# A 128x320 float32 memset on GpSimd behind each gather of an edge-featured message-passing layer

## The chip, the cores and the metric

The kernel runs on one core of a Trainium2 chip. The time is device microseconds of one execution, the median over runs. The engines are called as in the profile: PE (TensorE), PEld (its weight loads), DVE (VectorE), ACT (ScalarE), POOL (GpSimd) and SP (SyncE, which here only issues DMAs).

## The reference

A message-passing layer on a graph of N = 12,500 nodes and E = 800,000 edges, with 64 features per node, 4 per edge, and a hidden width H = 128. `src` and `dst` are random.

```
h_src = x[src]
h_dst = x[dst]
m_in = concatenate([h_src, h_dst, e_attr], axis=-1)     # 132 wide
h = silu(m_in @ w1 + b1)                                # 128 wide
msg = h @ w2 + b2                                       # 64 wide
return segment_sum(msg, dst, N)
```

## The kernel before

The node halves of `m_in @ w1` are made once: `Atab`, a table in DRAM with one row of 256 float16 numbers for each source node (512 bytes: two halves that are added up, for precision), and `Btab` in SBUF for the target nodes. For an edge there remain a row of `Atab`, a row of `Btab`, four edge features times a small matrix, the silu, and the sum by target. The product with `w2` is made after the sum, once for each node.

So that the sum needs no scatter, edges are put in order of their target first. `rank` works out each edge's place and `place` writes records of 16 edges to a DRAM buffer `buf` by an indirect DMA on GpSimd (the "scatter", L944 `buf<-cb,idx`, some 400 of them). The edges come in 16 portions; `rank` and `place` of the next portion run as a *filler* inside the main loop over the present one. The last portions' loop has no filler left.

The main loop (`run`) has 1590 iterations of 512 edges each, four tiles of 128. Work for one iteration is spread over several of them, with these lags: `load` of the records' target and source numbers 11 iterations ahead, `pairs` 10, `sources` (DVE makes the row numbers `ix`) 8, `gather` 6, `spread` 4, `targets` (ACT) 2, `marks` (DVE) 1, then in the iteration itself `pre` and `silu`, and `onehot` 1 and `seg` and `accum` 2 behind. In detail:

- `gather(n)`, L1155, issues four indirect DMAs on GpSimd's queue. Each fetches 128 rows of 512 bytes from `Atab` into `ga[:, t, :]`. `ga` has seven buffers (`NGA`), so the gather for iteration n + 6 needs the buffer that `pre(n - 1)` has read.
- `pre(n)` on PE: for each of the four tiles one matmul with the edge features (L1143) and two with `Btab` (L1145), then two of 512 columns that add the gathered rows by an identity matrix (L1147). All go into one PSUM bank `px`, of which there are three.
- `silu(n)` on ACT, L1166, reads `px` and writes `h`.
- `seg(n - 2)` on PE, L1174, sums `h` by target with a one-hot matrix `sg` (float32, made by ACT at L1162 from `ob`), into another `px`; `accum`, L1182, adds this on DVE to `S`.
- `targets`, L1118 and L1119 on ACT, and L1128 on DVE prepare the one-hot matrices, for two iterations at a time.

The filler's lines that show in the rows are L477, L492, L579, L583 and L591 (`rank`), L927 to L986 (`place`: DVE makes `mk` and `oh`, PE packs records in L983 and L986, ACT copies them to `cb` in L958, GpSimd scatters them).

The order of the work on each engine is the order in which the program is written; `in_order` sets what within an iteration goes first, on all engines alike. GpSimd does, in the main loop, nothing but the gathers and the scatters. DMAs on its queue take turns on eight semaphores, so that a DMA waits until the one eight places before it has landed.

Of the kernel before, what the change touches and what calls it, by code (L numbers as in the profile page):

```python
# [10 lines left out]
F32 = mybir.dt.float32  # L11
# [70 lines left out]
def tile_mpnn(ctx, tc, x, e_attr, src, dst, w1, b1, w2, b2, out, portions):  # L82
# [8 lines left out]
    VE, SC, GP, PE = nc.vector, nc.scalar, nc.gpsimd, nc.tensor  # L91
# [18 lines left out]
    cst = ctx.enter_context(tc.tile_pool(name="cst", bufs=1))  # L110
# [709 lines left out]
    def records(p, c0, cn):  # L820
# [53 lines left out]
        p["rec", c0] = (pay, lo, hv)  # L874
        yield 1200

    below = [zero[:, :CS * PC], zero[:, :CS * PC]]

    def place(p):
# [271 lines left out]
    def gather(n):  # L1151
        s = st[n]
        ga = wk.tile([128, 4, 2 * H], FH, name="ga", bufs=NGA)
        for t in range(4):
            GP.indirect_dma_start(out=ga[:, t, :], out_offset=None, in_=Atab,  # L1155
                                  in_offset=bass.IndirectOffsetOnAxis(ap=s["ix"][:, t:t + 1], axis=0))
        s["ga"] = ga

    def onehot(n):
# [33 lines left out]
    def run(m0, m1, filler):  # L1193
# [4 lines left out]
        for n in range(m0 - LL, m1 + 2):  # L1198
# [20 lines left out]
            if on(LG):  # L1219
                gather(n + LG)  # L1220
# [204 lines left out]
```

## Time and profile before

| | |
|---|---|
| median of three runs | 11,197.96 us (11,196.83 to 11,198.25) |
| span of the profiled execution | 11,179.7 us |
| that execution's time, with 18.3 us around the span as in the median | about 11,198 us |
| loop: first to last gather | 317.8 to 11,106.5 us |
| busy: PE, DVE, ACT, POOL | 73%, 57%, 35%, 58% |
| gathers | 6360, 951 ns mean |
| DMA, mean | 70 GB/s, 777 MB moved |

Before 317.8 us the tables and the first portion are made; behind the loop, some 70 us, the product with `w2` and the output. In the loop the profile shows the same picture slice by slice; up to about 1700 us DVE is the busiest engine, and from about 10,100 us on only gathers, `pre`, `silu`, `seg` and `accum` are left.

In a row of the time view the columns are: start in us, length, engine, line, operation, output and inputs, and in brackets the idle time of the engine before it with the instruction that ended it. "issue" means that the engine waited for nothing the profile shows, "remote" that the releaser isn't known. A row of a group has instructions, busy time, mean ns of one, then idle time before them and what ended it. In a row of a stretch each engine has its busy time and count, and then come the clock granted to PE, the DMA share and GB/s. The recorded ends of matmuls are modelled.

### The profile page before, as it was taken

Reading aid. Unit: us, or ns where it says so; the run is one execution under the profiler, and the core shown is the slowest. Engines: PE = TensorE matmul, PEld = TensorE weight load, DVE = VectorE, ACT = ScalarE, POOL = GpSimd, SP = SyncE. Lnnn points to the kernel's source line nnn. Section 1 sums busy time; section 2 is a strip of 40 time slices with the busy share of each in tenths; the row PEclk is TensorE's granted clock in tenths of the full one; section 3 lists DMA queues with packets and bytes.
Section 4 is the critical chain, followed back from the end, with each engine's and each line's share of the span. In section 5 each row is a group of like instructions: output and inputs, shape, how many; then the busy total and the mean of one; then the engine's idle time right before and its main releaser. Section 6 shows DMA issues by size and latency. Waiting matters only on the chain. (4 is left out here: it accounts for less than half of the span.)

```text
span 11179.7 us, 214957 instructions
## 1 busy us (share of the span) xinstructions
PE 8116.8 (73%) x73739; PEld 6653.7 (60%) x73739; DVE 6365.6 (57%) x18821; ACT 3859.6 (35%) x5331; POOL 6499.4 (58%) x6828
## 2 busy tenths in 40 slices
PE   7677777777777777777777777777777777775556
PEld 5566666666666566566566566666565565554445
DVE  8666676666665555555655555655555665441112
ACT  3233333333333333333333333333333333333333
POOL 1555555555555665566655666566566566666664
PEclk8777888888888778888888888888788887877777
DMA  2334434443443444444444444444444444444444
GB/s 92 64 66 72 67 58 71 65 73 64 72 66 64 76 67 66 76 68 67 77 66 66 76 68 66 74 69 68 75 67 66 74 67 69 69 67 71 72 72 68
DMA packets 3427360, 777.19 MB, mean 70 GB/s; under 512 B 3152950, under 2 KB 3215334, under 8 KB 3425036
## 3 DMA queue, kind: packets, MB, share of 16 engines
q1 hardware_dynamic: 3206638, 316.00, 26.1%
q0 software_dynamic: 218016, 446.07, 15.1%
q8 instruction: 645, 10.57, 0.4%
q14 instruction: 399, 3.27, 0.1%
q10 hardware_dynamic: 1662, 1.29, 0.0%
HBM read 712.51 MB, written 54.08 MB: 69 GB/s over the span
## 5 line engine op out<-in xcount | busy, mean ns | idle before, releaser
L1155 POOL DMA_INDIRECT ga<-Atab,ix x6360 | 6050.6, 951 | 4120.9 <-issue 1511.7
L1166 ACT ACTIVATE h<-px 128x512 f32<-128x512 f32 x1590 | 946.7, 595 | 6596.1 <-remote 2752.7
L1174 PE MATMUL px<-h,sg 128*128 128x129 f32 x12720 | 2375.2, 337 | 928.6 <-issue 387.7
L1174 PEld LDWEIGHTS px<-h,sg 128*128 128x128 f32 x12720 | 2065.8, 240 | 1155.0 <-issue 533.8
L983 PE MATMUL pl<-mk,oh 128*128 128x160 f16 x18750 | 1987.5, 260 | 575.8 <-issue 493.3
L983 PEld LDWEIGHTS <-oh 128*128 128x128 bf16 x18750 | 1637.8, 110 | 1037.3 <-issue 767.7
L1145 PE MATMUL px<-Btab,oT 128*128 x12720 | 1731.0, 249 | 159.4 <-issue 154.0
L1143 PE MATMUL px<-WE,pts 65*128 65x128 bf16 x6360 | 1489.0, 250 | 383.5 <-issue 241.1
L1182 DVE TENSOR_TENSOR S<-S,px 128x129 f32 x3180 | 906.2, 285 | 1341.2 <-remote 562.5
L1145 PEld LDWEIGHTS <-oT 128*128 128x128 bf16 x12720 | 1233.0, 114 | 575.1 <-issue 523.4
L930 DVE TENSOR_TENSOR mk<-fix,pay 128x320 int32<-128x320 int32 x1563 | 758.1, 485 | 1322.5 <-remote 712.0
L937 DVE TENSOR_TENSOR oh<-fix,lo 128x1536 bf16<-128x1536 bf16 x1563 | 1482.4, 948 | 0.1
L1147 PE MATMUL px<-ga,idA 128*128 128x512 f16 x3180 | 1172.0, 454 | 51.6 <-issue 46.2
L591 DVE TENSOR_REDUCE slT<-rx 128x5 f32<-128x490 f32 (+1 forms) x1302 | 833.2, 642 | 614.1 <-remote 305.1
L1119 ACT ACTIVATE oT<-oT,scl 128x1024 bf16<-128x1024 bf16 x795 | 986.1, 1240 | 26.7
L1162 ACT ACTIVATE sg<-ob 128x512 f32<-128x512 bf16 x1590 | 982.1, 618 | 0.0
L1118 ACT ACTIVATE oT<-oT,nip 128x1024 bf16<-128x1024 f16 x795 | 906.9, 1141 | 31.6 <-DMA oT<-dsc 24.7
L1143 PEld LDWEIGHTS <-pts 65*128 65x128 f16 x6360 | 722.2, 114 | 159.6 <-issue 113.1
L583 PEld LDWEIGHTS <-selB 99*128 99x128 bf16 x6250 | 479.1, 108 | 539.7 <-issue 428.3
L1128 DVE TENSOR_TENSOR ob<-fix,d 128x1024 bf16<-128x1024 bf16 x795 | 550.1, 692 | 352.3 <-ACT sg L1162 164.8
L583 PE MATMUL rx<-bT,selB 99*128 99x98 bf16 x6250 | 598.4, 224 | 198.1 <-issue 189.1
L579 PE MATMUL rx<-ohb,triO 128*128 128x490 bf16 (+1 forms) x1302 | 541.6, 416 | 120.5 <-DVE slT L591 49.8
(326 smaller groups left out, 5973.1 us busy)
## 6 DMA issues: line engine op xcount, KB each, us to landing
oT<-dsc SPq DMA_DIRECT2D x795, 256.0 KB
ga<-Atab,ix POOLq DMA_INDIRECT x6360
pts<-buf SPq DMA_DIRECT2D x2385, 16.0 KB
buf<-zero SPq DMA_DIRECT2D x184, 120.0 KB
dsc<-buf SPq DMA_DIRECT2D x795, 4.0 KB
pld<-dsc SPq DMA_DIRECT2D x795, 4.0 KB
Btab<-in_e_attr_dram POOLq DMA_DIRECT2D x10, 1250.0 KB
el<-in_e_attr_dram SPq DMA_DIRECT2D x74, 160.0 KB
```

Source lines behind the costliest of these rows:

```text
L583: PE.matmul(xp[:EP, i * R:(i + 1) * R], selB[:NR, s_:s_ + 1].to_broadcast([NR, EP]), bT[g][:NR, :R], start=False, stop=i == n - 1)
L937: VE.tensor_tensor(oh[:EP, :sn].rearrange("p s (j t) -> p s j t", t=2), io3[:EP].rearrange("p (j t) -> p j t", t=2).unsqueeze(1).to_broadc ...
L983: PE.matmul(pa[:, u * CS * PC:(u + 1) * CS * PC], oh_[:, u * 128:(u + 1) * 128], mv, start=s0 + i + u == 0, stop=False)
L1118: SC.activation(oT, oT.bitcast(FH), AF.Abs, bias=nip1[:, 0:1])
L1119: SC.activation(oT, oT, AF.Relu, scale=scl[:, 2:3], bias=inv)
L1143: PE.matmul(pr[:, sl], s["pts"][:, sl], WE, start=t == 0, stop=False)
L1145: PE.matmul(pr[:, sl], s["oT"][:, sl], Btab[:, ds(v[t // 2], 1), u, :], start=False, stop=False)
L1147: PE.matmul(pr.rearrange("p (t h) -> p t h", t=4), idA, s["ga"][:, :, u * H:(u + 1) * H], start=False, stop=u == 1)
L1155: GP.indirect_dma_start(out=ga[:, t, :], out_offset=None, in_=Atab, in_offset=bass.IndirectOffsetOnAxis(ap=s["ix"][:, t:t + 1], axis=0))
L1162: SC.activation(sg, s["ob"][:, :4].rearrange("p t h -> p (t h)"), AF.Copy)
L1166: SC.activation(hs[n % 3][:, :, :H], st[n]["pr"].rearrange("p (t h) -> p t h", t=4), AF.Silu)
L1174: PE.matmul(s["so"][t // 2], s["sg"][:, t * 128:(t + 1) * 128], hs[n % 3][:, t, :], start=t % 2 == 0, stop=t % 2 == 1)
```

## The change

A float32 tile of 128 partitions by 320 elements, `idle`, is added to SBUF, and behind each of the four indirect DMAs of `gather` GpSimd clears it. No instruction reads the tile. 6360 memsets are executed in all. Lines behind the first insertion move down by one, those behind the second by two: the gather is then L1156, the memset L1158.

```diff
@@ -874,6 +874,7 @@
         p["rec", c0] = (pay, lo, hv)
         yield 1200
 
+    idle = cst.tile([128, 320], F32, name="idle")
     below = [zero[:, :CS * PC], zero[:, :CS * PC]]
 
     def place(p):
@@ -1154,6 +1155,7 @@
         for t in range(4):
             GP.indirect_dma_start(out=ga[:, t, :], out_offset=None, in_=Atab,
                                   in_offset=bass.IndirectOffsetOnAxis(ap=s["ix"][:, t:t + 1], axis=0))
+            GP.memset(idle, 0.0)
         s["ga"] = ga
 
     def onehot(n):
```

## The prediction

> **What bounds the kernel now.** I read the page first (busy shares), then who waited for whom, then GpSimd's own rows in order of time, and last the sums by stage.
>
> ```profile
> PE 8116.8 (73%) x73739; PEld 6653.7 (60%) x73739; DVE 6365.6 (57%) x18821; ACT 3859.6 (35%) x5331; POOL 6499.4 (58%) x6828
> L1155 POOL DMA_INDIRECT ga<-Atab,ix x6360 | 6050.6, 951 | 4120.9 <-issue 1511.7 <-remote 862.2 <-PE px L1147 759.5
> L944 POOL DMA_INDIRECT buf<-cb,idx x407 | 413.7, 1016 | 305.4 <-ACT cb L958 181.9 <-issue 111.3 <-DMA Atab<-S 9.7
> L1155 POOL DMA_INDIRECT ga<-Atab,ix x6360: 942/947/1623, 317.8 to 11106.5; - x199
> ```
>
> No engine is full. The last row is of the gathers alone (min/median/max in ns, first and last start in us). The page would let GpSimd (POOL) be called idle 42% of the time, but of its idle time 1511.7 us is "issue", the gap that stands before nearly every gather and in which nothing else can start. The gathers run from 317.8 to 11106.5 us: 10,789 us for 1590 iterations, 6.79 each. The waits:
>
> ```profile
> ACT h L1166 <- remote: 2752.7, 611, 10.0
> ACT h L1166 <- PE px L1147: 1959.4, 344, 26.3
> POOL ga L1155 <- issue: 1511.7, 4896, 4.9
> POOL ga L1155 <- remote: 862.2, 545, 3.0
> POOL ga L1155 <- PE px L1147: 759.5, 235, 11.4
>   PEld L1147: 4.8, 8
>   PE px L1147: 3.6, 4
> ```
>
> The last two rows are from the gather's line, of those who waited for it: nearly nobody, 12 times in 6360. So the gathered data is always early, six iterations ahead. The rows above say the opposite of GpSimd: 4896 gathers follow the one before them on the queue, and the other 6360 - 4896 = 1464 had to be let go by another engine. That makes 1464 bursts of DMAs with a pause behind each. Bursts of four, five (the fifth is a scatter of the filler) and eight, in GpSimd's rows by time (start, length, engine and line, idle time before):
>
> ```profile
> 6002.61 0.97 POOL L1155 DMA_INDIRECT ga<-Atab,ix  x1 [1.38 <-PE rx L583]
> 6003.88 0.95 POOL L1155 DMA_INDIRECT ga<-Atab,ix  x1 [0.30 <-issue]
> ...
> 6006.38 0.94 POOL L1155 DMA_INDIRECT ga<-Atab,ix  x1 [0.30 <-issue]
> 6008.77 0.94 POOL L1155 DMA_INDIRECT ga<-Atab,ix  x1 [1.45 <-PE pl L983]
> ...
> 6014.84 0.95 POOL L1155 DMA_INDIRECT ga<-Atab,ix  x1 [1.37 <-remote]
> ...
> 6019.84 1.01 POOL L944 DMA_INDIRECT buf<-cb,idx  x1 [0.30 <-issue]
> 6022.27 0.97 POOL L1155 DMA_INDIRECT ga<-Atab,ix  x1 [1.42 <-remote]
> ...
> 6082.04 0.95 POOL L1155 DMA_INDIRECT ga<-Atab,ix  x1 [1.35 <-remote]
> ...
> 6090.79 0.94 POOL L1155 DMA_INDIRECT ga<-Atab,ix  x1 [0.30 <-issue]
> 6093.88 0.94 POOL L1155 DMA_INDIRECT ga<-Atab,ix  x1 [2.14 <-remote]
> ...
> 10919.07 0.95 POOL L1155 DMA_INDIRECT ga<-Atab,ix  x1 [0.31 <-issue]
> 10922.06 0.95 POOL L1155 DMA_INDIRECT ga<-Atab,ix  x1 [2.04 <-remote]
> ...
> 10930.82 0.95 POOL L1155 DMA_INDIRECT ga<-Atab,ix  x1 [0.30 <-issue]
> 10933.76 0.94 POOL L1155 DMA_INDIRECT ga<-Atab,ix  x1 [1.99 <-remote]
> ```
>
> Inside a burst the starts are 1.25 us apart (0.95 + 0.30). From the start of a burst to the start of the next: four DMAs 6.16 and 6.07 us, five 7.43, eight 11.84, and eight in the tail 11.70. Four DMAs more cost 11.84 - 6.07 = 5.77, so 1.44 us for each, not 1.25, and T(n) = 1.44 n + 0.32 fits all (6.08, 7.52, 11.84). Over the loop it gives (6360 + some 380 scatters) x 1.44 + 1464 x 0.32 = 10,170 of the 10,789 us, 94%. So the loop keeps the time of GpSimd's DMAs, at 1.44 us each, though GpSimd itself shows 1.25. What lies between is in the next rows, of the last stretch, where the filler is over:
>
> ```profile
> 10919.58 0.59 PE L1147 MATMUL px<-ga,idA 128*128 128x512 f16 x2
> 10921.82 0.60 ACT L1166 ACTIVATE h<-px 128x512 f32<-128x512 f32 x1 [7.31 <-remote]
> 300.00:1700.00 1400.00, 1033.37 (x10345) 857.56 (x10343) 956.86 (x2961) 439.21 (x600) 770.25 (x807) 0.80 0.40 66
> 10300.00:11100.00 800.00, 451.42 (x3041) 385.09 (x3038) 153.28 (x493) 296.83 (x405) 513.23 (x542) 0.73 0.48 72
> ```
>
> TensorE (PE) is recorded to end the pre-activations at 10920.17, yet ACT's silu, which needs them, starts at 10921.82, and the next burst of gathers, which needs the same signal (the buffer is free), 0.24 us after the silu. The signal comes only 2.75 us after the last DMA of the burst has started (10919.07). In the last row, of the tail, PE is busy 451 of 800 us, DVE 153, ACT 297, POOL 513: nobody is full, and the period still follows the count of DMAs. The trace does not show what holds PE's signal back during a burst; it shows by how much. The first row of the two, 300 to 1700 us, is the one stretch where DVE is busier (957 of 1400 us) than POOL.
>
> **The change part by part.** 1. One tile of 320 float32 in each partition is added in SBUF; nothing reads it, so no engine gains a wait for it. 2. 6360 memsets are added on GpSimd's queue. On that queue, in the middle of the loop, the gathers of an iteration and the first of the next stood thus (a wait for DMASW is for the DMA eight places back, for PE_49 the buffer's last reader):
>
> ```order
> L1155 DMA ga<-Atab,ix 128x256 [waits DMASW3_49,PE_49]
> L1155 DMA ga<-Atab,ix 128x256 [waits DMASW4_49]
> L1155 DMA ga<-Atab,ix 128x256 [waits DMASW5_49]
> L1155 DMA ga<-Atab,ix 128x256 [waits DMASW6_49]
> L1155 DMA ga<-Atab,ix 128x256 [waits DMASW7_49,DVE_49,PE_49]
> ```
>
> and stand now, with a scatter (L945) behind them:
>
> ```order
> L1156 DMA ga<-Atab,ix 128x256 [waits DMASW1_49,DVE_49,PE_49]
> L1158 MEMSET idle 128x320 [waits Pool_49]
> L1156 DMA ga<-Atab,ix 128x256 [waits DMASW2_49]
> L1158 MEMSET idle 128x320 [waits Pool_49]
> L1156 DMA ga<-Atab,ix 128x256 [waits DMASW3_49]
> L1158 MEMSET idle 128x320 [waits Pool_49]
> L1156 DMA ga<-Atab,ix 128x256 [waits DMASW4_49]
> L1158 MEMSET idle 128x320 [waits Pool_49]
> L945 DMA buf<-cb,idx 76544x160 [waits DMASW5_49,Activation_49]
> ```
>
> Nothing changes places; a memset stands between any two gathers, and it waits only for the memset before it, which was done a whole DMA earlier. Behind it on the queue wait the next gather or the scatter. The price of a memset is bounded by GpSimd's own:
>
> ```profile
> L356 POOL MEMSET sg<- 1x512 f32 x24 | 12.8, 537 | 138.6 <-PE px L362 134.6 <-PE fix L193 3.9
> L356 POOL MEMSET sg<- 1x256 f32 x1 | 0.3, 306 | 3.3 <-PE px L362 3.3
> L373 POOL MEMSET S<- 128x1806 f32 x7 | 11.3, 1609 | 0.4
> 260.98 0.97 POOL L944 DMA_INDIRECT buf<-cb,idx  x1 [9.65 <-DMA Atab<-S]
> 261.99 1.61 POOL L373 MEMSET S<- 128x1806 f32 x1
> 0.30 0.12 POOL L1409 MEMSET const-bfloat16-1.0<- 128x1 bf16 x1
> 0.33 0.12 POOL L1409 MEMSET const-uint8-127<- 128x1 uint8 x1
> ```
>
> From 256 to 1806 elements is 1.303 us, 0.84 ns for an element, so 320 take 0.306 + 64 x 0.84 ns = 0.36 us (by the 512 row at most 0.37). 6360 of them are 2,280 us of GpSimd. A memset begins 0.04 us behind a DMA (261.95 to 261.99). What the trace never shows is a DMA that is ready behind a memset. The spacing s of gathers is then, as a low bound, 0.95 + 0.04 + 0.36 = 1.35, if the 0.30 of "issue" passes while the memset runs (the last two rows show such overlap: memsets of 0.12 us start 0.03 apart); as a high bound that plus 0.30, 1.65. I take 1.25 + 0.355 = 1.605: the gap stands before each indirect DMA but not before a memset, so it seems to belong to the DMA's own start.
>
> The forecast rests on what 1.605 does to the 1.44. It is more than 1.44, so DMAs no longer pile up. What held PE's signal is then the last DMA alone: T'(n) = (n-1) s + 1.44 + 0.32. Against T(n) each burst loses (n-1)(s - 1.44), and over the loop that is the 4896 gathers that follow another: 4896 x 0.165 = +808 us. From that I take off the stretch up to 1700 us, where DVE is fuller than POOL: 807 of 6828 GpSimd instructions, 12%. That leaves +711; the memset behind the last gather of a burst costs nothing, since it lies in the pause (1.4 to 2.1 us idle); if the pause went, it would cost its 0.36 as well, 1464 x 0.36 = 527. PE does not wait for later data: a whole burst that is late by 1.4 us comes out of a lead of six iterations, some 40 us. What is late next is the silu, which the pause feeds, and behind it PE's segment sums and DVE's adds.
>
> The profiled span is 11,179.7 us and the median of the runs 11,198; the 18.3 lie around the span and are kept. 11,198 + 711 = 11,909; I say 11,900.
>
> One more cost is possible. 300 to 1700 us holds some 750 gathers; if each memset held DVE up by its full 0.36 whenever DVE is busy (957/1400 = 0.68), the stretch would grow by 750 x 0.36 x 0.68 = +184. I leave it out: the gathers' 942/947/1623 shows a median 5 ns over the minimum beside a DVE that is busy 57%, so nothing on GpSimd is being held by DVE as a rule. The Trainium skill's page "SBUF — State Buffer" (section "SBUF: two separate sides") does say that GpSimd and a DVE instruction in a two-port mode exclude each other for a whole instruction; by that rule the sum would be nearer 12,090, and no row here shows such a hold on either side.
>
> **The rivals.** R1, all of it adds: PE's signal waits for GpSimd's whole chain, and each memset lengthens it. For: the 1.44 is more than GpSimd's own 1.25, so there is a serial thing that POOL's time may be added to. Against: the 0.19 that it exceeds looks like a second, parallel limit. 4896 x 0.36 = 1,760 (the last of a burst hidden) to 6360 x 0.36 = 2,290, less 12%: +1,550 to +2,010, 12,750 to 13,210.
>
> R2, the other side: with s over 1.44 there is a short calm behind each DMA, PE's signal slips through within the burst, and the pauses of 1.4 to 2.1 us go. GpSimd then runs without a break: 4 x 1.605 + 0.256 x 1.31 (407 scatters over 1590 iterations) = 6.76 per iteration, 10,740 us for 10,789 now: -50, 11,150. It decides at s = 1.61: below, faster (at 1.55, -400 at most, if PE and DVE can follow), above, slower (at 1.65, +235). Small waits that remain would push it up. For: a lone DMA is no pile. Against: in the tail each burst holds the signal although PE is recorded to have ended 1.65 us before.
>
> R3, no change: s is 1.35 to 1.44, the memset lies in the issue gap, and the 1.44 per DMA goes on setting the period: 11,198, up to +100.
>
> R4: the memset costs far more beside DVE or beside a descriptor write than alone: over 0.5 us each, above 13,200.
>
> **How the numbers follow.** Forecast 0.38; R1 0.20; R2 0.20, half of it below zero; R3 0.15; R4 0.07. Faster by over 0.2% (22 us, about what can be told from no change): 0.10, from R2. Within 0.2%: R3 mostly, and a little of R2, 0.13. Slower: 0.77. The forecast alone, with s from 1.54 to 1.65, is 4896 x 0.88 x (0.10 to 0.21) = +430 to +905, 11,630 to 12,100. The range for 8 in 10 runs from 11,130 (most of R2) to 13,000 (the lower half of R1).
>
> **What would show it.** GpSimd's rows: gather to gather 1.6 us with a memset of 0.36 behind each. Right: bursts of four take 6.5 to 6.6 us, eight 13.0, pauses remain, and silu starts some 1.7 us after the last gather. R1: four take 7.2 or more. R2: pauses vanish, the "remote" and PE waits before the gather fall to a few hundred us, and POOL is busy 75% or more of the span. R3: spacing 1.35 to 1.44 and bursts of four still 6.1. The prediction is wrong if memsets are longer than 0.4 us, if the gap before a gather shrinks, or if PE's signal no longer follows the DMAs.

## The result and the profile after

The changed kernel takes 10,956.7 us (10,948 to 10,966, four runs) where the kernel before takes 11,198.1 us: ratio 0.979, interval 0.978 to 0.980. It is 2.1% faster. The forecast was 11,900 us, slower, in a range that began at 11,130. Of all executions in this document one is left out of its ratio, as far slower than the others of its kernel: 16,097 us, of `w360` below.

The page's first row and the groups of GpSimd in the kernel after:

```profile
span 10946.3 us, 221318 instructions
PE 8233.5 (75%) x73739; PEld 6563.2 (60%) x73739; DVE 6642.0 (61%) x18821; ACT 3876.8 (35%) x5331; POOL 8972.5 (82%) x13188
L1156 POOL DMA_INDIRECT ga<-Atab,ix x6360 | 6100.6, 959 | 1491.9 <-issue 924.3 <-PE px L1148 253.2 <-remote 82.0
L1158 POOL MEMSET idle<- 128x320 f32 x6360 | 2438.4, 383 | 4.7
```

GpSimd's busy time grew by 2,473 us, nearly all of it the memsets, and its idle time before gathers fell by 2,629 us, from 4,120.9 to 1,491.9. So more idle time went than the memsets cost. Of it 587 us is "issue" (1511.7 to 924.3), a gap that is shorter behind a memset; the rest is pauses that other engines end, and these are the part to read: "remote" was 862.2 and is 82.0, PE's `px` was 759.5 and is 253.2. The waits, of GpSimd and of PE, in the kernel after:

```profile
POOL ga L1156 <- issue: 924.3, 5444, 4.9
POOL ga L1156 <- PE px L1148: 253.2, 150, 9.7
ACT h L1168 <- remote: 1466.4, 326, 15.4
PE px L1148 <- DMA ga<-Atab,ix: 407.4, 157, 6.2
```

5444 gathers now follow the one before on the queue, so 6360 - 5444 = 916 had to be let go by another engine, for 1464 before. Most of the 916 hardly wait: counted in the traces, waits of over 0.6 us before a DMA of this queue fell from 1368 to 257. The last row is new: PE waits for gathered data, 157 times. GpSimd has become the bound in a part of the loop. GpSimd's rows in the middle of the loop and in the tail:

```profile
6007.44 0.95 POOL L1156 DMA_INDIRECT ga<-Atab,ix  x1 [0.33 <-PE rx L783]
6008.40 0.38 POOL L1158 MEMSET idle<- 128x320 f32 x1
6008.94 0.95 POOL L1156 DMA_INDIRECT ga<-Atab,ix  x1 [0.16 <-issue]
6009.89 0.38 POOL L1158 MEMSET idle<- 128x320 f32 x1
6010.43 0.95 POOL L1156 DMA_INDIRECT ga<-Atab,ix  x1 [0.16 <-issue]
...
6013.43 1.00 POOL L945 DMA_INDIRECT buf<-cb,idx  x1 [0.17 <-issue]
6014.74 0.96 POOL L1156 DMA_INDIRECT ga<-Atab,ix  x1 [0.30 <-issue]
...
6021.06 0.95 POOL L1156 DMA_INDIRECT ga<-Atab,ix  x1 [0.49 <-remote]
...
10600.31 0.95 POOL L1156 DMA_INDIRECT ga<-Atab,ix  x1 [0.16 <-issue]
...
10606.29 0.95 POOL L1156 DMA_INDIRECT ga<-Atab,ix  x1 [0.16 <-issue]
```

Gathers start 1.495 us apart: 0.95, a memset of 0.38, and a gap of 0.16 that was 0.30 between two DMAs. The burst of five (6007.44 to 6014.74) takes 7.30 us, for 7.43 before, with no wait behind its scatter; the burst of four behind it 6.32, for 6.07 to 6.16. The tail runs at GpSimd's own 5.98 us an iteration, a little slower than before (11.70 / 2 = 5.85).

The plainest place is the first burst of the loop, 16 gathers in a row, while PE and DVE work on `rank` beside it: PE writes `rx` (L583), DVE reduces it (L591). In the kernel before:

```profile
326.46 0.61 PE L583 MATMUL rx<-bT,selB 99*128 99x98 bf16 x5
327.05 0.67 DVE L591 TENSOR_REDUCE slT<-rx 128x5 f32<-128x490 f32 x1 [1.41 <-PE rx L583]
328.13 0.61 PE L583 MATMUL rx<-bT,selB 99*128 99x98 bf16 x5
335.59 0.67 DVE L591 TENSOR_REDUCE slT<-rx 128x5 f32<-128x490 f32 x1 [7.55 <-issue]
336.31 0.57 PE L579 MATMUL rx<-ohb,triO 128*128 128x490 bf16 x1 [7.56 <-DVE slT L591]
336.67 0.61 PE L583 MATMUL rx<-bT,selB 99*128 99x98 bf16 x5
340.52 0.67 DVE L591 TENSOR_REDUCE slT<-rx 128x5 f32<-128x490 f32 x1 [3.94 <-remote]
```

and in the kernel after:

```profile
325.37 0.61 PE L583 MATMUL rx<-bT,selB 99*128 99x98 bf16 x5
326.09 0.66 DVE L591 TENSOR_REDUCE slT<-rx 128x5 f32<-128x490 f32 x1
326.27 0.61 PE L583 MATMUL rx<-bT,selB 99*128 99x98 bf16 x5
327.06 0.66 DVE L591 TENSOR_REDUCE slT<-rx 128x5 f32<-128x490 f32 x1
328.13 0.61 PE L583 MATMUL rx<-bT,selB 99*128 99x98 bf16 x5
328.85 0.66 DVE L591 TENSOR_REDUCE slT<-rx 128x5 f32<-128x490 f32 x1
```

The matmuls that end at 328.74 are seen by DVE at 335.59 before and at 328.85 after, in the middle of the same burst. PE is not behind with its own work there: it stands idle for 7.56 us, waiting for DVE. The other way round there is no delay: DVE's reduction ends at 336.26 and PE starts at 336.31. What comes late, when GpSimd's gathers follow each other at 1.25 us, is what PE signals.

The traces also record when a semaphore changed, for nine in ten of PE's signals and for about half of DVE's and ACT's. From 330 us on, the recorded signals of DVE come 0.011 us and those of ACT 0.009 us (medians) behind the end of an instruction that signals, in both kernels; those not recorded can't be judged by this. Those of PE come 1.06 us behind it in the median before and 0.56 after; 28% are over 2 us late before, 14% after, and 22% and 23% come within 0.05 us. So the change shortens the hold on PE's signals and does not end it.

### The profile page after: what moved, and what is told of

The parts are those of the page before. It is cut to its first block, busy times and chain, and to the rows that moved or that the text cites. A ratio compares the mean times of both kernels' runs of the same rounds, so it can differ in the third digit from the quotient of the medians.

```text
span 10946.3 us, 221318 instructions
## 1 busy us (share of the span) xinstructions
PE 8233.5 (75%) x73739; PEld 6563.2 (60%) x73739; DVE 6642.0 (61%) x18821; ACT 3876.8 (35%) x5331; POOL 8972.5 (82%) x13188
## 5 line engine op out<-in xcount | busy, mean ns | idle before, releaser
L1156 POOL DMA_INDIRECT ga<-Atab,ix x6360 | 6100.6, 959 | 1491.9 <-issue 924.3
L1176 PE MATMUL px<-h,sg 128*128 128x129 f32 x12720 | 2328.7, 333 | 368.2 <-issue 181.6
L1158 POOL MEMSET idle<- 128x320 f32 x6360 | 2438.4, 383 | 4.7
L1176 PEld LDWEIGHTS px<-h,sg 128*128 128x128 f32 x12720 | 2040.5, 237 | 576.5 <-issue 336.4
L984 PEld LDWEIGHTS <-oh 128*128 128x128 bf16 x18750 | 1589.1, 109 | 891.6 <-issue 594.2
L1146 PE MATMUL px<-Btab,oT 128*128 x12720 | 1771.7, 247 | 155.4 <-issue 142.5
L591 DVE TENSOR_REDUCE slT<-rx 128x5 f32<-128x490 f32 (+1 forms) x1302 | 834.0, 642 | 630.7 <-PE px L1148 241.3
L583 PEld LDWEIGHTS <-selB 99*128 99x128 bf16 x6250 | 458.9, 105 | 497.6 <-issue 381.6
```

The costliest lines, as they stand in the source:

```text
L984: PE.matmul(pa[:, u * CS * PC:(u + 1) * CS * PC], oh_[:, u * 128:(u + 1) * 128], mv, start=s0 + i + u == 0, stop=False)
L1146: PE.matmul(pr[:, sl], s["oT"][:, sl], Btab[:, ds(v[t // 2], 1), u, :], start=False, stop=False)
L1158: GP.memset(idle, 0.0)
L1176: PE.matmul(s["so"][t // 2], s["sg"][:, t * 128:(t + 1) * 128], hs[n % 3][:, t, :], start=t % 2 == 0, stop=t % 2 == 1)
```

## The experiments

Each was timed against the kernel before on its own chip; ratios are to that.

**The width of the memset.** Theory A: the spacing of the gathers is what counts. Theory B: any instruction behind a DMA lets the signals out.

```diff
-    idle = cst.tile([128, 320], F32, name="idle")
+    idle = cst.tile([128, 1], F32, name="idle")        # w1; 160, 240, 480, 360 in the others
```

> The memset clears 128x1 instead of 128x320; 6360 of them as before. Theory A (spacing): what helps is that the starts of two gathers lie 1.495 us apart and no longer 1.25, longer than the 1.44 us per DMA by which PE's signals were held. A memset of 0.1 us leaves the spacing at 1.20 to 1.30, so DMAs pile up as in the kernel before: 11,150 to 11,230 us, bursts of four 6.1 us from start to start. Theory B (presence): any ordinary instruction behind a DMA lets PE's signals out, whatever its length. Then the gain stays or grows, since GpSimd is less busy: under 10,960.

> The memset clears 128x160, about 0.24 us: spacing some 1.35 us, below 1.44. Theory A: the pile-up per DMA halves (0.19 to 0.09 us), so the time lies between both kernels, 11,050 to 11,180, nearer the kernel before. Theory B: at or below the changed kernel, under 10,960.

> The memset clears 128x240, about 0.31 us: spacing some 1.42 us, just below 1.44. Theory A: nearly no pile-up and 0.075 us less of GpSimd's time for each gather than in the changed kernel; 10,870 to 11,000. Theory B: under 10,950, in line with the smaller widths (no step between the widths).

> The memset clears 128x480, about 0.53 us: spacing 1.64 us. GpSimd alone then needs 4 x 1.64 + 0.256 x 1.31 = 6.90 us for an iteration, 10,960 us for the loop, and some 400 us lie around the loop: both theories expect GpSimd to be the bound, 11,350 to 11,550. If it stays under 11,200 the count of GpSimd's time is wrong.

One chip, 11,204 us before. Spacing is the median from start to start of two gathers; pauses are GpSimd's waits "remote" and for `px`, in us (the pauses of the first row and the whole row at 320, the changed kernel, are from the first result):

| kernel | memset | spacing | pauses | time | ratio (interval) |
|---|---|---|---|---|---|
| before | none | 1.25 | 862 + 760 | 11,204 | 1 |
| w1 | 0.12 | 1.25 | 926 + 937 | 11,255 | 1.005 (1.003 to 1.006) |
| w160 | 0.25 | 1.36 | 416 + 812 | 11,235 | 1.003 (1.002 to 1.004) |
| w240 | 0.32 | 1.43 | 249 + 563 | 11,128 | 0.994 (0.992 to 0.995) |
| 320 | 0.38 | 1.50 | 82 + 253 | 10,957 | 0.979 (0.978 to 0.980) |
| w480 | 0.52 | 1.63 | 0 + 13 | 11,304 | 1.009 (1.008 to 1.011) |

Theory B is out: w1 has all 6360 memsets and no gain. From w1 on the pauses shrink with the spacing, step by step. None of the four fell into its range: w1 (11,230 at most) and w160 and w240 (11,180 and 11,000 at most) came out slower than theory A had said, w480 a little faster than its 11,350. At spacings of 1.36 and 1.43 us the wider spacing costs GpSimd time and gives hardly anything. At w480 GpSimd hardly pauses (13 us) and PE waits for data, the reverse of the kernel before:

```profile
PE px L1148 <- DMA ga<-Atab,ix: 2671.2, 899, 10.1
POOL ga L1156 <- issue: 1005.7, 5903, 0.4
```

There PE's signals come 0.014 us behind its instructions in the median, and 79% within 0.05 us: between 1.50 and 1.63 us of spacing the hold goes nearly whole, but by then GpSimd's own time is the bound.

**One partition instead of 128.**

```diff
-            GP.memset(idle, 0.0)
+            GP.memset(idle[0:1, :], 0.0)
```

> The changed kernel with the memset on one partition, 1x320 instead of 128x320: 128 times less written into SBUF. If GpSimd's time for it is the same 0.36 to 0.38 us, the spacing is 1.49 and theory A (spacing alone) expects the ratio of the changed kernel, 0.975 to 0.983. If it is the write into 128 partitions that matters (a port, a drain of earlier writes), the ratio is over 0.99.

0.985 (0.984 to 0.987), between the two ranges that were expected. The memset takes 0.357 us instead of 0.383, and the spacing is 1.47 instead of 1.50, which puts it between w240 and the changed kernel, as do its pauses (144 + 426 us). So the write into 128 partitions isn't needed for a gain. That the 0.6% less than in the changed kernel is due to 0.03 us of spacing isn't shown: the two ran on two chips.

**Where the memsets stand.** `three` and `three400` leave out the one behind the fourth gather, `last` has that one alone, `pair` every second.

```diff
-            GP.memset(idle, 0.0)
+            if t < 3:                  # last: t == 3, 1152 wide; pair: t % 2, 640 wide
+                GP.memset(idle, 0.0)   # three400: 400 wide
```

> The changed kernel without the memset behind the fourth gather of an iteration: 4770 memsets of 128x320. Theory A: the three gaps within a group are calm (1.495 us), one is 1.25, so at most 0.19 us piles up in a group and is drained in the next; signals come as early as in the changed kernel and GpSimd has 0.24 us less for each iteration, so that stretches where GpSimd is the bound (the tail, 5.98 to 6.00 us there) fall to 5.75 to 5.9. Ratio 0.970 to 0.981. Against it: if every DMA needs its calm, ratio 0.985 to 1.0.

> As the one before, with 128x400: three gaps of about 1.565 and one of 1.25, 5.95 us for an iteration, nearly GpSimd's time of the changed kernel. If the calm within a group is what counts and more of it is better (1.565 against 1.495), it beats the changed kernel: ratio 0.965 to 0.978. If calm beyond 1.5 brings nothing: 0.978 to 0.985.

> The changed kernel, with one memset of 128x1152 behind the fourth gather of an iteration only: about GpSimd's time of four memsets of 288, but the four gathers stand 1.25 us apart as before. Theory A in its strict form (it is the spacing between any two DMAs that counts): signals are held through a group as before, and the memset lies in the pause; 11,100 to 11,300. Theory A': what counts is that DMAs do not pile up over groups; the memset of 1.0 us drains the pile of four, and the time is within 60 us of the changed kernel, 10,900 to 11,020. Theory B: one instruction for each group, nearly no gain, over 11,150.

`three` 0.986 (0.985 to 0.988), `three400` 0.977 (0.976 to 0.979, 10,945 us), `last` 0.995 (0.994 to 0.997). GpSimd gets some 1.1 us of memset an iteration in `last` and in `three`; behind the fourth gather it brings 0.5%, spread over the gaps 1.4%. These two ran on different chips, and the chip matters (below), so the place of the memset is not shown to be the reason. `three` and `three400` ran on one chip: gaps of 1.56 us for 1.49 take another 1% off, with as many memsets. `three400` is as fast as the changed kernel with fewer of them. `three` missed the range of theory A and fell into the one against it, 0.985 to 1.0: the one gap of 1.25 us seems to cost more than the saved memset brings.

**What the 1.44 us depend on**, in the kernel without memsets: bytes, rows, buffers, and PE's own work.

```diff
# half: 256 bytes a row
-            GP.indirect_dma_start(out=ga[:, t, :], out_offset=None, in_=Atab,
+            GP.indirect_dma_start(out=ga[:, t, :H], out_offset=None, in_=Atab.rearrange("n (u h) -> (n u) h", u=2),
# rows64: 64 rows a DMA
+            GP.indirect_dma_start(out=ga[:64, t, :], ... ap=s["ix"][:64, t:t + 1]
# deep
-NGA = 7
+NGA = 9                      # and the gathers 8 iterations ahead
# segh
-        t = cst.tile([128, 4, H + 1], F32, name=f"h{i}")
+        t = cst.tile([128, 4, H + 1], FH, name=f"h{i}")      # and sg
```

> The kernel before (no memset), with gathers of 128 rows of 256 bytes instead of 512: the table is read as rows of half the length, which fetches other numbers than the layer needs, and PE adds the one half twice, so its work stays. If the 1.44 us per DMA is the transfer of 64 KB, it falls to 0.8 to 1.0 us, below GpSimd's 1.25, nothing piles up, the pauses shrink, and the time is 10,600 to 10,950. If it is the making or handling of 128 descriptors, 1.44 us stays and so does the time, 11,100 to 11,210. Theory C (PE's own backlog) expects no change as well.

> The kernel before (no memset) with gathers of the first 64 rows of each tile, and PE adds those 64 alone: half of the edges lack their source term; the count of DMAs, of matmuls and of columns stays. If the 1.44 us are made by the 128 descriptors, they halve, nothing piles up, and bursts of four take under 5.6 us: ratio under 0.96 (GpSimd's own time for a DMA may fall too). If they belong to the DMA as such, T stays 6.1 and the ratio is 0.995 to 1.005.

> The kernel before (no memset), with nine gather buffers instead of seven and gathers 8 iterations ahead instead of 6 (and the steps that feed them two earlier). If the bursts pause because a buffer is late, two more buffers take the pause away: under 11,000. Theory A: the pause follows PE's signal, which comes when the DMAs have drained, and buffers change nothing: 11,150 to 11,260.

> The kernel before (no memset), with the one-hot matrix and h of the segment sums in float16 instead of float32, which lowers their precision and PE's work. Theory A (PE's signals are held by the gathers' DMAs, PE itself has time to spare): the law of 1.44 us per DMA stays, bursts of four 6.1 us, time 11,050 to 11,210. Theory C (PE's records run ahead of the array; the float32 matmuls of the segment sums take longer than recorded, and the late signals are PE's own backlog): the signals come earlier by what is saved, over 1 us for an iteration, and the time falls below 10,400.

| kernel | T(4), T(8) in us, medians | ratio (interval) |
|---|---|---|
| before, chip of the first result | 6.10, 11.90 | 1 |
| half | 6.18, 12.02 | 1.000 (0.999 to 1.001) |
| rows64 | 6.09, 11.90 | 1.006 (1.004 to 1.008) |
| deep | 6.18, 12.01 | 1.000 (1.000 to 1.001) |
| segh | 6.17, 11.97 | 0.988 (0.986 to 0.989) |

(half, deep and segh ran on a chip where the kernel before takes 11,342 us, rows64 where it takes 11,203.) In all of them four more DMAs cost 5.8 us, 1.45 each. The length of a burst with its pause goes by the count of DMAs, whatever their rows or bytes. In rows64 GpSimd's own spacing falls to 1.21 us and the bursts keep their length; its time is just over the expected 1.005. More buffers bring nothing. And PE is not its own brake: half-width operands in the segment sums bring PE's busy time to 7,533 us, from 8,180 in `deep` on the same chip, and take 1.2% off the time, and leave the length of the bursts alone.

Nor do the transfers pile up. By the packet records of the kernel before, in the middle of its loop, a gather has landed 2.57 us (median) after its start as the first of a burst of up to eight, 2.23 as the fourth and 2.20 as the eighth. What grows is the time from the last landing to the start of the next burst: 0.11 us behind four DMAs, 0.98 behind eight.

**A chip without the hold.** Three kernels were sent to learn more, and came on a chip on which the kernel before takes 8,966 us.

> The changed kernel with the segment sums in float16, as in segh (lower precision, less PE work). If the gathers' spacing still holds PE's signals in the changed kernel, less PE work brings no more than the 1.25% it brought without the memset: ratio to the kernel before 0.965 to 0.979. If PE's own work is what the changed kernel waits for now, it falls further, towards GpSimd's 4 x 1.495 + 0.335 = 6.33 us for an iteration: ratio under 0.962.

> The changed kernel with 128x360: spacing some 1.535 us. GpSimd's least time for an iteration is 6.47 us, for the changed kernel's 6.32 and its measured 6.6 in the middle. If more calm still frees signals there, ratio 0.968 to 0.977 with the tail slower (6.14 us); if GpSimd's time already counts in full, 0.985 to 0.995.

> The changed kernel with 128x640 behind every second gather instead of 128x320 behind each: the same GpSimd time to within 0.1 us for an iteration, mean spacing near 1.5, but in pairs 1.25 apart with 1.8 behind. If the mean spacing counts, the ratio is that of the changed kernel, 0.975 to 0.985. If each DMA needs its own calm, only half of the places for a signal are there: 0.985 to 1.0 (the memset behind four gathers brought 0.995).

`segh_m` 10,467 us, `w360` 10,683, `pair` 10,525; ratios 1.167 (1.165 to 1.169), 1.191 (1.189 to 1.194) and 1.174 (1.172 to 1.176). None of the expected ratios came true, since all of them rest on a kernel before of some 11,200 us. The expectations' own sums still hold: 6.33 us of GpSimd's time for an iteration of `segh_m` is 10,060 us for the loop, and with some 400 around it 10,460. `segh_m`'s row shows GpSimd with hardly a pause for others:

```profile
POOL 1788888888888888888888888888888888888886
POOL ga L1156 <- issue: 1003.6, 5895, 0.5
```

The kernel before fits the same sum with 1.25 us: 4 x 1.25 + 0.256 x 1.31 = 5.34 us, 8,480 us, and with 400 around it 8,880 of the 8,966. So on that chip GpSimd's queue seems to be the plain bound, and memsets are paid for in full. For the kernel before this is a sum: it was only timed there, not profiled, and the changed kernel not run. For the three with memsets the traces show that the hold is absent: PE's signals come 0.014 us behind its instructions in the median, over 99% within 0.05 us, at a spacing of 1.49 us in `segh_m` and in pairs 1.25 us apart in `pair`. Of the signals of all three engines 98% or more are recorded there. The granted clock does not tell the chips apart: 0.75, 0.82 and 0.83 in these three, 0.73 (`segh`) to 0.82 (the changed kernel) where the hold is.

**Once more.** The last three came on a fifth chip.

> The kernel before, unchanged, with a profile on this chip. Where it takes about 8,970: GpSimd's gathers in long bursts 1.25 us apart with hardly a pause, silu within 0.1 us of the recorded end of its matmuls, and 4 x 1.25 + 0.256 x 1.31 = 5.34 us for an iteration. Where it takes 11,200: the rows of the first profile, T(4) 6.1 us and silu 2.9 us late.

> The changed kernel once more, on whichever chip comes up. On three chips the kernel before took 11,200 to 11,340 us, on a fourth 8,966. Where it takes about 11,200: PE's signals are held there, ratio 0.975 to 0.985. Where it takes about 8,970: they are not held, GpSimd is the bound in both kernels, and 6360 gathers 0.245 us further apart cost 1,560 us: 10,420 to 10,520 us, ratio 1.16 to 1.175.

> 128x640 behind every second gather, on this chip. Where the kernel before takes 11,200: if the mean spacing counts, 0.975 to 0.985; if each DMA needs its own calm, 0.985 to 1.0. Where it takes 8,970: GpSimd's time again, 10,480 to 10,560 us, ratio 1.17 to 1.18, and nothing is learnt on the spacing.

The kernel before takes 11,329 us, and its waits are those of the first profile:

```profile
POOL ga L1155 <- issue: 1514.5, 4896, 8.1
POOL ga L1155 <- remote: 942.3, 561, 2.9
POOL ga L1155 <- PE px L1147: 795.1, 229, 11.9
```

The changed kernel has 0.992 (0.990 to 0.993) there, faster but outside the expected range: pauses of 142 + 398 us are left, for 82 + 253. Bursts of eight less bursts of four are 12.00 - 6.18 = 5.82 us on this chip, 1.455 us per DMA, and its spacing is 1.494, so the calm is 0.04 us where the first chip had 1.498 - 1.45 = 0.05. Whether that is the whole of the difference isn't shown. `pair` has 0.989 (0.987 to 0.990), at least as good as a memset behind each. By its ranges that reads "each DMA needs its own calm", but the ranges took the changed kernel at 0.975 to 0.985, and here it has 0.992. So not every gap has to be calm; a memset behind every second DMA does as well on this chip. Behind every fourth (`last`) it seems not to (0.995, on a chip of much the same time), though the mean spacing of both is 1.5 us.

`pair` is the one kernel with a memset that was traced on both kinds of chip. PE's last addition of gathered rows and the silu that reads it, first where the kernel before takes 8,966 us, then where it takes 11,329:

```profile
4890.43 0.59 PE L1148 MATMUL px<-ga,idA 128*128 128x512 f16 x2
4891.06 0.60 ACT L1169 ACTIVATE h<-px 128x512 f32<-128x512 f32 x1 [4.42 <-PE px L1148]
5541.02 0.59 PE L1148 MATMUL px<-ga,idA 128*128 128x512 f16 x2
5543.95 0.60 ACT L1169 ACTIVATE h<-px 128x512 f32<-128x512 f32 x1 [3.62 <-PE px L1177]
```

ACT stood idle both times when the matmuls ended. The silu starts 0.04 us behind them on the one chip and 2.34 on the other; the medians over the silus for which ACT stood idle are 0.04 and 1.75.

## Why the prediction was wrong

- **What bounds the kernel** was read rightly in its time: 1.44 us per DMA, beyond GpSimd's own 1.25, with PE's signals late. Bytes, rows, buffers and PE's work were each ruled out, by a run, as what sets the 1.44. The picture behind it, DMAs that pile up, is not borne out: the eighth gather of a burst lands no later after its start (2.20 us) than the first (2.57). What is late is PE's signal.
- **The memset's price.** Bounded by 0.36 to 0.37, it took 0.383 beside the DMAs: 6360 x 0.383 = 2,438 us.
- **The spacing.** I took 1.605 between the bounds 1.35 and 1.65, on the reading that the whole 0.30 gap belongs to the DMA's start. It is 1.495: behind a memset only 0.165 of the 0.30 gap is left, so other work can start in that gap, against what I said of it; in w1 a memset of 0.12 us fits into it, and the spacing stays 1.25. The overlap that spoke for the low bound was in the rows I quoted, and a gap that shrinks was one of my signs of being wrong.
- **The step that failed** is the one behind it: "What held PE's signal is then the last DMA alone", with a pause of the old length behind every burst. Put 1.495 into that formula and it still says slower: 4896 x 0.055 x 0.88 = +237 us. In its place most of the pauses went: waits of over 0.6 us fell from 1368 to 257, "remote" and `px` together from 1,622 us to 335. PE's signals came out within the bursts, 0.56 us late in the median after 1.06, not behind each burst's last DMA.
- **PE and its data.** "PE does not wait for later data" failed as well, in a small way: PE now waits 157 times for a gather, 407 us in all.
- **R2** had the mechanism, at a chance of 0.20, and its break-even, s = 1.61, fits: 1.50 is faster, 1.63 (w480) slower. By its sum s = 1.495 would give 4 x 1.495 + 0.335 = 6.32 us an iteration, 10,040 us for the loop. Measured are 10,886.3 - 317.5 = 10,569, so 220 of 750 us came. The rest are largely pauses that remain (1491.9 - 924.3 = 568 us before gathers): where ACT stands idle when the matmuls end, silu still starts 1.33 us behind them in the median, after 2.07. w360, which should have told how much more calm would bring, fell on the chip without the hold; this stays open.
- **R1** is out: a chain of DMA and memset that adds would have made bursts of four 7.2 us; without a wait they take 6.32. **R3** is out for this width; w160, with a spacing of 1.36 us and a ratio of 1.003, is what it describes. **R4** is out by 0.383 against 0.5.
- **DVE and the memset.** I had priced this at up to 184 us and left it out. DVE's casts (L1126 before, L1127 after), 16 elements wide, are held up by the memset:

```profile
L1126 DVE CAST d<-pld 128x16 bf16<-128x16 f16 x795 | 151.5, 191 | 0.0
L1127 DVE CAST d<-pld 128x16 bf16<-128x16 f16 x795 | 239.1, 301 | 0.0
L1127 DVE CAST d<-pld 128x16 bf16<-128x16 f16 x795 | 161.3, 203 | 0.0
L938 DVE TENSOR_TENSOR oh<-fix,lo 128x1536 bf16<-128x1536 bf16 x1562 | 1482.4, 949 | 0.1
```

The rows are of before, after, p1, and after again. The cast grows from 191 to 301 ns; the long comparison with two inputs keeps its 949. The Trainium skill's page "SBUF — State Buffer" (section "SBUF: two separate sides") says so: a DVE instruction in a two-port mode and a GpSimd instruction exclude each other, one with two inputs and a GpSimd instruction that reads nothing do not. The trace agrees in these two groups; which mode an instruction runs in it does not show. A memset of one partition, 0.357 us long, costs the cast only 12 ns. The sum is small: DVE's busy time grew by 276 us in all, and the first stretch, where DVE is fullest, became faster all the same: the first 800 gathers and scatters took 1,330 us, after 1,378.

## What to carry to other kernels

A queue that has idle time in the profile can be the cause of a wait that the profile puts on another engine: when an engine's bursts have a length that follows the count of its instructions and not the others' work, test the spacing of that engine before its load. Where a wait is released late and everybody who waits is released together, a pause put between the suspected instructions is a cheap test, and one partition of a memset is enough (1.5% here). The traces' records of semaphores tell directly whose signals are late. Before such padding is kept, time it on several chips: here it gains 2.1% on one and 0.8% on another, and by the runs with other paddings would cost about 17% on a third.

## What was not expected of the hardware

- PE's signals come late while indirect DMAs from GpSimd's queue follow each other at 1.25 us: 1.06 us in the median, where DVE's and ACT's recorded ones come within 0.011. A burst with its pause takes 1.44 to 1.46 us more for each DMA, for 64 or 128 rows, 256 or 512 bytes. At 1.50 us the median is 0.56, at 1.63 us 0.014. What in the chip holds them isn't shown by any trace here.
- The kernel before takes 8,966 us on one chip and 11,203, 11,204, 11,329 and 11,342 us on four others (medians; 11,198 in the first result). The profiles of those where it takes 11,200 or more show the hold; on the other, three kernels with memsets were traced and show none (0.014 us). That the kernel before lacks it there too is inferred, not traced.
- An indirect DMA behind a memset starts 0.165 us after it (0.19 behind the shortest, of 0.12 us), behind another DMA 0.30.
